# Row stores before the q and k loads, gate steps moved forward on VectorE, first weight loads on GpSimd's queue

## The chip, the cores and the metric

The program runs on one core of a Trainium2 chip. The metric is the device time of one execution in microseconds (us), as the median of several executions. A core has five engines that run their own instruction streams and meet only at semaphores: TensorE (PE in the profile: matmuls and transposes; PEld is its loading of weights), VectorE (DVE), ScalarE (ACT), GpSimd (POOL) and SyncE (SP, which does nothing here but read registers, branch and start DMAs). DMAs are started by SP and by POOL; SP's travel on one DMA queue, POOL's on another.

## The reference

Three layers follow each other. Sliding-window attention over 4 batches, 8 heads, 576 positions (heads 0 to 3 with a plain window of 32, heads 4 to 7 with a window of 128 dilated by 4); a mixture of 8 experts in which each of the 2304 tokens goes to the one expert with the highest logit; and a dense layer with a rational function between its two products.

```python
def _attn_ref(q, k, v):
    scores = scale * np.matmul(q, k.transpose(0, 1, 3, 2))
    scores = np.where(masks[None, :, :, :], scores, -1000000000.0)
    attn = np.exp(scores - np.max(scores, axis=-1, keepdims=True))
    attn = attn / (np.sum(attn, axis=-1, keepdims=True) + 1e-09)
    return np.matmul(attn, v)

def _moe_ref(x, modality_id, w_gate, modality_bias, w1, w2):
    logits = x @ w_gate + modality_bias[modality_id]
    e_idx = np.argmax(logits, axis=1)
    probs = softmax(logits)                      # gate_w = the chosen expert's share
    for e in range(8):
        mask = e_idx == e
        h = np.maximum(x[mask] @ w1[e], 0.0)
        out[mask] = gate_w[mask, None] * (h @ w2[e])
    return out

def _moe2_ref(x, w_in, w_out, a, b):
    h = x @ w_in
    P = a[0] + a[1] * h + a[2] * h**2 + a[3] * h**3
    Q = 1.0 + np.abs(b[0]) * np.abs(h) + np.abs(b[1]) * h**2
    return (P / (Q + 1e-06)) @ w_out
```

## The kernel before

**Order.** Instructions are written by hand in the order in which each engine runs them; the framework only adds the semaphores. What an engine finds blocked holds up everything behind it on that engine.

**Attention (`fused`).** Eight chunks of two heads by two batches (kinds dilated, dilated, plain, plain, twice) pass through 36 groups `g` of four tiles. For each group PE makes scores (`step_s`, tile `sc`), transposes the exponentials (`step_t`, `pt`) and multiplies them with v (`step_v`, `pv`, one PSUM buffer); VectorE divides and writes the rows into `xu` (L545). A tile `xu` holds two chunks, and there are two such tiles, so the first write of the third pair of chunks waits until every DMA that stores the first tile has read it. `load(c)` brings q and k of a chunk (`ldq`, `ldk`, two buffers each) by four DMAs on SP. `put_x` stores a finished `xu` to `x_rows` in DRAM: for a dilated pair of chunks by 20 small DMAs, which are put into the list `slow`; the loads of dilated v go into the list `first`. `issue(PACE)` at the end of each group starts up to four entries of the lists, those of `first` ahead. So the place of a store on SP, before or behind the four loads of the next chunk, is set by how many groups have passed.

**Experts (`moe`).** The tokens, sorted by expert, are run through slots of 128. A slot `s` gathers its rows on POOL (`gather`, L942, tiles `xg`), multiplies with w1 (`stage_1`, `p1t`), transposes (`stage_t`, `pht`) and multiplies with w2 (`stage_2`, `pot`); ScalarE's `put` scales `pot` by `gate` into `yo` and SP stores it to `ys_rows` (L1079). Matmuls are done in three products of high and low halves (`w1h`, `w1l` and so on). Where the expert changes between slots, `swap1` and `swap2` split new weights, the third quarter of each on POOL; where it doesn't, each engine walks past the branch. Three places of this part are in the change:

- Behind the fourth to eighth low half of w2 (`lo2`, list `lows`) VectorE writes the first two rows of the slot table `tab` (L974 to L1004). The generator `gates` (L951 to L969: 12 steps on VectorE and one on POOL, which make the three parts `ag` of the gate weights) is taken up step by step later, between the steps that write the rest of `tab` (L1251 to L1282). `followers` (L1285) comes behind these; then `gates_pe` (L1062) brings `ag` into slot order by 18 matmuls into `pyt` and VectorE combines them into `gate`. On PE these 18 stand behind 18 of the 24 matmuls of slot 2's first stage.
- Experts with few tokens left over are served at the side (`side`): their weights `sw` come by `side_fetch`, 8 DMAs of 256 KB for each matrix, and their rows go out by `side_put` (L1238), a scatter on POOL that waits for the latest store to `ys_rows`. Where `side_fetch` has nothing to fetch, SP, before it passes, waits until the eight semaphores over which its DMAs rotate have all been reached.
- The weights of the dense layer come as 64-bit numbers and are turned into 32-bit ones between slots (`narrow`, L1101: one ScalarE step and three VectorE steps for each of 32 pieces). `narrow_in` (L1094) loads a piece of 512 KB into `dr`, one of two buffers; the next piece is asked for as soon as VectorE has freed the buffer. All of these loads stand on SP.

**Dense layer (`second`).** 80 units of 512 columns; nothing in it is changed.

Of the kernel before, what the change touches and what calls it, by code (L numbers as in the profile page):

```python
# [2 lines left out]

# [9 lines left out]
I32 = mybir.dt.int32  # L13
# [152 lines left out]
def fused(ctx, tc, io):  # L166
# [214 lines left out]
    with ExitStack() as actx, tc.manual_schedule(), nc.allow_low_precision(reason="integers"):  # L381
# [24 lines left out]
        def load(c):  # L406
            bp, _, kind, h0 = CHUNKS[c]
            raw[c] = [ld.tile([72, 2, 2, 8 * D] if kind else [QT, 2 * NJ, 2, D], F32, tag="ld" + nm, name="ld" + nm) for nm in "qk"]
            bs = slice(2 * bp, 2 * bp + 2)
            if c == 0:  # L410
                for hh in range(2):
                    for t, src, eng in zip(raw[c], (q, k), (nc.sync, nc.scalar)):
                        eng.dma_start(out=t[:, hh], in_=src[bs, h0 + hh].rearrange("b (p j) d -> p b (j d)", j=8))
                    if hh == 0:
                        nc.sync.dma_start(out=ident, in_=io["cst"][:, 0:128])
                for lo, hi in ((0, 2), (2, NP0)):
                    nc.scalar.dma_start(out=mask[:, lo:hi], in_=io["mask"][:, lo:hi])
# [233 lines left out]
        for g in range(NG):  # L651
# [39 lines left out]
            if done_T == 4 * NU and not w1s:  # L691
# [7 lines left out]
                for n in range(2):  # L699
                    fetch2(n, e)  # L700
            if done_L < NC and done_T >= 8 * (done_L - 1):
                load(done_L)
                done_L += 1
            if done_V < done_L and TPG * (g - LAG2 + 1) >= 2 * NJ * (done_V // 2 * 2 - 2):
                load_values(done_V)
                first.append(lambda c=done_V: halo(c))
                done_V += 1
            issue(PACE)

        def split1(n, eng=nc.gpsimd):  # L710
            nonlocal nsp
# [35 lines left out]
def moe(ctx, tc, io, sh):  # L747
# [222 lines left out]

    gq = gates()
    lows = (lo2(c) for c in range(4, 8))
    cn = cd[0:1]
    nc.vector.tensor_tensor(out=cd[:, 0, :], in0=cnt, in1=nt[:, 0, :], op=ALU.min)  # L974
    next(lows, None)
    sd = st[0:1]
    S8 = [1, NS, 8]
    slot = C("slot")[0:1, 0:NS].rearrange("p (s o) -> p s o", o=1)
    wv = T([1, 1, 8], name="wv")
    nc.vector.scalar_tensor_tensor(out=wv, in0=cn, scalar=0.0, in1=nfe[0:1], op0=ALU.is_gt, op1=ALU.mult)  # L980
    next(lows, None)
    ge = T(S8, name="ge")
    es = T([1, NS, 1], name="es")
    nc.vector.memset(es[:, 0:1, :], 0.0)
    ge1 = ge[:, 1:]
    S7 = [1, NS - 1, 8]
    nc.vector.scalar_tensor_tensor(out=ge1, in0=slot[:, 0:NS - 1].to_broadcast(S7), scalar=128.0, in1=sd.to_broadcast(S7), op0=ALU.mult, op1=ALU.is_ge)
    next(lows, None)
    nc.vector.tensor_tensor(out=ge1, in0=ge1, in1=wv.to_broadcast(S7), op=ALU.mult)
    next(lows, None)  # L990
    nc.vector.tensor_reduce(out=es[:, 1:, 0], in_=ge1, op=ALU.max, axis=AX.X)
    next(lows, None)
    nc.vector.tensor_tensor(out=ge, in0=wv.to_broadcast(S8), in1=es.to_broadcast(S8), op=ALU.is_gt)
    next(lows, None)
    nc.vector.tensor_tensor(out=tab[:, 0, 0:NS - 1], in0=es[:, 1:, 0], in1=es[:, 0:NS - 1, 0], op=ALU.not_equal)
    next(lows, None)
    nc.vector.tensor_tensor(out=ge, in0=ge, in1=C("rev")[0:1, :].rearrange("p (o e) -> p o e", o=1).to_broadcast(S8), op=ALU.mult)
    next(lows, None)
    nx = T([1, NS], name="nx")
    nc.vector.tensor_reduce(out=nx, in_=ge, op=ALU.max, axis=AX.X)  # L1000
    next(lows, None)
    nc.vector.tensor_scalar(out=nx, in0=nx, scalar1=-1.0, scalar2=8.0, op0=ALU.mult, op1=ALU.add)
    next(lows, None)
    nc.vector.tensor_scalar(out=tab[:, 1, :], in0=nx, scalar1=7.0, scalar2=None, op0=ALU.min)  # L1004
    next(lows, None)
    run(lows)
    fill(slot1, 16 - FB)
    fill(second0, 8)
    run(slot1)
# [84 lines left out]
    def narrow_in(i):  # L1094
        qd, which, kk = i // 8, i // 4 % 2, i % 4
        w32[i] = pools["pa"].tile([128, 512], I32, tag="w" if i < 16 else "u", name=f"w32_{i}", bufs=17 if i < 16 else 16)
        r = pools["dp"].tile([128, 512, 2], I32, tag="dr", name="dr")
        nc.sync.dma_start(out=r, in_=srcs[which][qd, kk].bitcast(I32).rearrange("p (f w) -> p f w", w=2))
        nar[i] = r

    def narrow(chunks, ahead):  # L1101
# [147 lines left out]
    vs = T([1, NS], name="vs")  # L1249
    en = T([1, 1, 8], name="en")  # L1250
    nc.vector.tensor_tensor(out=en, in0=sd, in1=nt[0:1], op=ALU.add)  # L1251
    next(gq, None)
    nc.vector.tensor_reduce(out=tot, in_=en, op=ALU.max, axis=AX.XY)
    next(gq, None)
    nc.vector.tensor_scalar(out=vs, in0=slot[:, :, 0], scalar1=128.0, scalar2=tot, op0=ALU.mult, op1=ALU.is_lt)
    next(gq, None)
    nc.vector.tensor_copy(out=tab[:, 2, :], in_=vs)
    next(gq, None)
    nc.vector.scalar_tensor_tensor(out=ge, in0=slot.to_broadcast(S8), scalar=128.0, in1=sd.to_broadcast(S8), op0=ALU.mult, op1=ALU.subtract)
    next(gq, None)  # L1260
    nc.vector.scalar_tensor_tensor(out=ge, in0=ge, scalar=0.0, in1=cn.to_broadcast(S8), op0=ALU.max, op1=ALU.min)
    next(gq, None)
    cb = T([1, NS], name="cb")
    nc.vector.tensor_reduce(out=cb, in_=ge, op=ALU.add, axis=AX.X)
    next(gq, None)
    nc.vector.tensor_tensor(out=vs[:, 0:NS - 1], in0=cb[:, 0:NS - 1], in1=vs[:, 0:NS - 1], op=ALU.mult)
    next(gq, None)
    nc.vector.tensor_reduce(out=cb[:, NS - 1:], in_=vs[:, 0:NS - 1], op=ALU.max, axis=AX.X)
    next(gq, None)
    ct = T([128, 1, 8], name="ct")  # L1270
    nc.vector.tensor_tensor(out=ct[:, 0, :], in0=cnt, in1=cd[:, 0, :], op=ALU.subtract)
    next(gq, None)
    tt = T([1, 1], name="tt")
    nc.vector.tensor_reduce(out=tt, in_=ct[0:1, 0, :], op=ALU.add, axis=AX.X)
    next(gq, None)
    nc.vector.tensor_scalar(out=tab[:, 3, 0:2], in0=cb[:, 0:2], scalar1=tt, scalar2=None, op0=ALU.add)
    nc.vector.tensor_scalar(out=tab[:, 3, 2:], in0=cb[:, 2:], scalar1=tt, scalar2=hole[0:1], op0=ALU.add, op1=ALU.add)
    next(gq, None)
    nc.vector.memset(tab[:, 4, :], 0)
    nc.vector.tensor_scalar(out=tab[:, 4, 0:8], in0=ct[0:1, 0, :], scalar1=0.0, scalar2=None, op0=ALU.is_gt)  # L1280
    next(gq, None)
    nc.vector.tensor_reduce(out=tab[:, 4, 9:11], in_=tab[:, 4, 0:8].rearrange("p (c e) -> p c e", c=2), op=ALU.max, axis=AX.X)  # L1282
    next(gq, None)

    def followers():  # L1285
        tv, tq, tm = T([1, 1, 8], name="tv"), T([1, 8, 8], name="tq"), T([1, 8], name="tm")
# [389 lines left out]
```

## Time and profile before

| | |
|---|---|
| Executions timed | 823.46, 825.47, 827.88 us; median 825.47 us |
| Profiled execution | 818.36 us, of which the span from first to last instruction is 816.5 us |
| PE | 784.9 us busy, 96% of the span |
| DVE, ACT, POOL | 576.2 us (71%), 509.5 us (62%), 140.2 us (17%) |
| Mean granted TensorE clock | 0.984 of full speed |
| DMA | 91.60 MB; 69587 packets of SP's queue, 3360 of POOL's |

The rows below come from one profiled execution. In a timeline a row gives the start of an instruction, its duration, the engine, the line of the kernel, the operation and its tiles; the brackets give how long the engine had been idle before it and which event ended that. "SPq" and "POOLq" are the sequencers of these engines. The rows of windows give how long each engine was busy in a stretch, the granted clock of TensorE as a share of its full speed, the share of time in which the 16 DMA engines worked, and GB/s.

### The profile page before, as it was taken

The numbers are of one execution on the slowest core, as the hardware profiler recorded it, in microseconds if no ns is written. First come the engines' busy times: TensorE is split into PE (matmuls) and PEld (weight loads), VectorE is DVE, ScalarE is ACT, GpSimd is POOL, SyncE is SP. The second block draws the span as 40 slices with busy tenths as digits, with TensorE's granted clock in tenths as the row PEclk, the third lists the DMA queues.
The fourth block names the chain that finished last, engine by engine and source line by source line (L and its number), as shares of the span: only waits on it lengthen the run. The fifth ranks groups of instructions, "written<-read, shape, count | busy, mean of one in ns | idle before, by whom it ended". The sixth has DMA issues, their size and how long they took to land.

```text
span 816.5 us, 15443 instructions
## 1 busy us (share of the span) xinstructions
PE 784.9 (96%) x5297; PEld 636.8 (78%) x5299; DVE 576.2 (71%) x1389; ACT 509.5 (62%) x993; POOL 140.2 (17%) x181
## 2 busy tenths in 40 slices
PE   8998899989999999999899999999999999999995
PEld 4766666777776878888678888888888889999884
DVE  2776789742243235894599988888788788888894
ACT  3666567323343343664699877766777778778783
POOL 2030004131102002230366502000020002001001
PEclk7999899999999999999999999999999999999998
DMA  7988946479778947781011001100020001001001
GB/s 187 161 168 156 178 155 196 141 253 319 248 265 277 322 148 250 259 293 55 17 40 42 12 0 65 40 0 1 1 90 1 1 1 64 1 1 39 1 0 39
DMA packets 73654, 91.60 MB, mean 112 GB/s; under 512 B 33721, under 2 KB 43467, under 8 KB 73547
## 3 DMA queue, kind: packets, MB, share of 16 engines
q1 hardware_dynamic: 69587, 78.48, 33.5%
q0 software_dynamic: 3360, 11.03, 3.9%
q8 instruction: 49, 0.80, 0.4%
q10 hardware_dynamic: 600, 0.81, 0.4%
q14 instruction: 58, 0.48, 0.2%
HBM read 75.59 MB, written 14.71 MB: 111 GB/s over the span
## 4 chain that ended last, share of the span: by engine, by line
PE 66%; DVE 1%; ACT 1%; issue 1%; POOL 0%; POOLq 0%; ACTq 0%
PE p1t L1407 8%; PE p1t L1408 8%; PE p1t L1409 8%; PE pht L1578 4%; PE pht L1577 4%; PE pht L1579 4%; PE pot L797 3%; PE pot L799 2%; PE pot L795 2%; PE pot L1579 2%; PE p1t L149 2%; PE p1t L147 2%; PE p1t L145 2%; PE pxt L1577 2%; PE pxt L1578 2%; PE pxt L1579 2%
## 5 line engine op out<-in xcount | busy, mean ns | idle before, releaser
L1525 ACT ACTIVATE raw<-p1t 128x512 f32<-128x512 f32 (+1 forms) x78 | 43.2, 554 | 82.4 <-PE p1t L1409 82.4
L1532 DVE TENSOR_TENSOR raw<-raw,raw 128x512 f32<-128x512 f32 (+1 forms) x80 | 51.9, 648 | 58.4 <-ACT raw L1526 57.6
L1409 PE MATMUL p1t<-yh,wl 128*128 128x512 f32 (+1 forms) x240 | 88.9, 370 | 0.0
L788 DVE TENSOR_TENSOR hl<-pht,hh 128x512 fp32r<-128x512 f32 x34 | 21.9, 686 | 82.3 <-ACT hh L787 82.1
L1526 ACT ACTIVATE raw<-raw,bab 128x512 f32<-128x512 f32 (+1 forms) x80 | 61.9, 774 | 2.7
L1588 POOL DMA_INDIRECT out<-hs,row x10 | 10.8, 1084 | 302.1 <-ACT hs L1586 300.7
L1407 PE MATMUL p1t<-yh,wh 128*128 128x512 f32 (+1 forms) x160 | 59.6, 372 | 0.3 <-DVE m L1543 0.3
L1408 PE MATMUL p1t<-yl,wh 128*128 128x512 f32 (+1 forms) x160 | 59.2, 370 | 0.0
L1554 DVE SCALAR_TENSOR_TENSOR m<-m,nab,raw 128x512 f32<-128x512 f32 (+1 forms) x80 | 58.6, 733 | 0.1
L1552 DVE SCALAR_TENSOR_TENSOR raw<-raw,raw 128x512 f32<-128x512 f32 (+1 forms) x80 | 56.3, 704 | 0.0
L1527 ACT ACTIVATE raw<-p1t,nab 128x512 f32<-128x512 f32 (+1 forms) x78 | 56.1, 719 | 0.0
L145 PE MATMUL p1t<-w1h,xh 128*128 128x512 f32 x136 | 55.1, 405 | 0.0
L797 PE MATMUL pot<-w2l,hh 128*128 128x512 f32 x128 | 51.0, 399 | 3.2 <-POOLq L1037 3.2
L1534 ACT ACTIVATE raw<-raw,bab 128x512 f32<-128x512 f32 (+1 forms) x80 | 53.7, 671 | 0.4 <-DVE raw L1532 0.3
L147 PE MATMUL p1t<-w1l,xh 128*128 128x512 f32 x136 | 53.7, 395 | 0.3 <-DVEq L1029 0.3
L149 PE MATMUL p1t<-w1h,xl 128*128 128x512 f32 x136 | 53.8, 396 | 0.1
L1543 DVE SCALAR_TENSOR_TENSOR m<-m,nab,p1t 128x512 f32<-128x512 f32 (+1 forms) x78 | 53.4, 685 | 0.1
L1550 DVE SCALAR_TENSOR_TENSOR raw<-raw,raw 128x512 f32<-128x512 f32 (+1 forms) x80 | 52.7, 659 | 0.0
L1541 DVE TENSOR_TENSOR m<-raw,p1t 128x512 f32<-128x512 f32 (+1 forms) x78 | 49.3, 632 | 3.3 <-PE pdt L824 0.7
L795 PE MATMUL pot<-w2h,hh 128*128 128x512 f32 x128 | 51.5, 402 | 0.0
L799 PE MATMUL pot<-w2h,hl 128*128 128x512 f32 x128 | 50.2, 392 | 0.0
L1409 PEld LDWEIGHTS p1t<-yh,wl 128*128 128x128 f32 x240 | 45.0, 188 | 6.3
(391 smaller groups left out, 2083.7 us busy)
## 6 DMA issues: line engine op xcount, KB each, us to landing
sw<-in_w SPq DMA_DIRECT2D x80, 256.0 KB
raw<-in_w SPq DMA_DIRECT2D x12, 1024.0 KB
dr<-in_w_in SPq DMA_DIRECT2D x16, 512.0 KB
dr<-in_w_out SPq DMA_DIRECT2D x16, 512.0 KB
y<-ys_rows SPq DMA_DIRECT2D x18, 256.5 KB
ldq<-in_q SPq DMA_DIRECT2D x16, 288.0 KB
ys_rows<-yo SPq DMA_DIRECT2D x17, 256.5 KB
ldk<-in_k SPq DMA_DIRECT2D x14, 288.0 KB
```

The costliest lines, as they stand in the source:

```text
L145: nc.tensor.matmul(out=p, lhsT=xh[:, kk], rhs=wh[n][:, kk], start=(kk == 0), stop=False)
L147: nc.tensor.matmul(out=p, lhsT=xh[:, kk], rhs=wl[n][:, kk], start=False, stop=False)
L149: nc.tensor.matmul(out=p, lhsT=xl[:, kk], rhs=wh[n][:, kk], start=False, stop=(kk == 3))
L795: nc.tensor.matmul(out=p, lhsT=a[:, c], rhs=w2h[n][:, kk], start=(c == 0), stop=False)
L797: nc.tensor.matmul(out=p, lhsT=a[:, c], rhs=w2l[n][:, kk], start=False, stop=False)
L799: nc.tensor.matmul(out=p, lhsT=b[:, c], rhs=w2h[n][:, kk], start=False, stop=(c == 7))
L1407: nc.tensor.matmul(out=p[:, 0:n], lhsT=wh(kk)[:, cs], rhs=ab[0][:, kk, 0:n], start=(kk == 0), stop=False)
L1408: nc.tensor.matmul(out=p[:, 0:n], lhsT=wh(kk)[:, cs], rhs=ab[1][:, kk, 0:n], start=False, stop=False)
L1409: nc.tensor.matmul(out=p[:, 0:n], lhsT=wl(kk)[:, cs], rhs=ab[0][:, kk, 0:n], start=False, stop=(kk == 3))
L1526: nc.scalar.activation(out=v, in_=ah, func=AF.Identity, scale=bab[:, 1:2], bias=bab[:, 0:1])
L1554: nc.vector.scalar_tensor_tensor(out=m, in0=m, scalar=nab[:, 0:1], in1=v, op0=ALU.add, op1=ALU.mult)
L1579: nc.tensor.matmul(out=o, lhsT=gl[:, cs], rhs=wa, start=False, stop=(f == 15))
```

## The change

Four edits, in three places.

- In attention, when the next chunk's q and k are about to be loaded and at most `FLUSH` = 5 entries are left in `slow`, all entries of both lists are started first. And a group in which both lists have entries starts six of them and not four.
- The generator `gates` is chained behind the last low halves of w2, so its steps stand between the steps that write the first two rows of `tab`; the rest of it follows right behind them. The later steps of `tab` are left alone among themselves. `ct` is computed at the start.
- `narrow_in` starts the loads of pieces 0 to 15 on POOL's queue; pieces 16 to 31 stay on SP.

```diff
+FLUSH = 5
...
             if done_L < NC and done_T >= 8 * (done_L - 1):
+                if len(slow) <= FLUSH:
+                    issue(len(first) + len(slow))
                 load(done_L)
...
-            issue(PACE)
+            issue(PACE + 2 if first and slow else PACE)
...
     gq = gates()
     lows = (lo2(c) for c in range(4, 8))
+    both = iter(chain(lows, gq))
+
+    def more():
+        next(both, None)
+
     cn = cd[0:1]
     nc.vector.tensor_tensor(out=cd[:, 0, :], in0=cnt, in1=nt[:, 0, :], op=ALU.min)
-    next(lows, None)
+    ct = T([128, 1, 8], name="ct")
+    nc.vector.tensor_tensor(out=ct[:, 0, :], in0=cnt, in1=cd[:, 0, :], op=ALU.subtract)
+    more()
...
-    next(lows, None)
-    run(lows)
+    more()
+    run(both)
...
-        nc.sync.dma_start(out=r, in_=srcs[which][qd, kk].bitcast(I32).rearrange("p (f w) -> p f w", w=2))
+        (nc.gpsimd if i < 16 else nc.sync).dma_start(out=r, in_=srcs[which][qd, kk].bitcast(I32).rearrange("p (f w) -> p f w", w=2))
...
     nc.vector.tensor_tensor(out=en, in0=sd, in1=nt[0:1], op=ALU.add)
-    next(gq, None)
     nc.vector.tensor_reduce(out=tot, in_=en, op=ALU.max, axis=AX.XY)
-    next(gq, None)
...
-    run(gq)
     followers()
     gates_pe()
```

On SP, in attention, the 20 stores of the first `xu` stand with the loads of the sixth and seventh chunk. Near the end of these stores the order was, before:

```order
L437 DMA x_rows<-xu 64x256
L437 DMA x_rows<-xu 48x256
L425 DMA ldq<-in_q 64x18x64 x2
L425 DMA ldk<-in_k 64x18x64 x2
L437 DMA x_rows<-xu 16x256
L437 DMA x_rows<-xu 64x2x256
L609 DMA x_rows<-xu 64x9x256 x2
```

and is now:

```order
L439 DMA x_rows<-xu 64x256
L439 DMA x_rows<-xu 48x256
L439 DMA x_rows<-xu 16x256
L439 DMA x_rows<-xu 64x2x256
L427 DMA ldq<-in_q 64x18x64 x2
L427 DMA ldk<-in_k 64x18x64 x2
L611 DMA x_rows<-xu 64x9x256 x2
```

The last two stores of the tile have moved in front of the four loads. In the same way the loads of the chunk before, which stood behind the third of the 20 stores, now stand behind the ninth.

On VectorE, where the later rows of `tab` are written (`g`, `pc` and `ag` belong to the gates, the others to the table), the order was, before:

```order
L955 TENSOR_SCALAR g<-g 128x18
L1255 TENSOR_SCALAR vs<-cst,tot 1x26
L957 RECIPROCAL g<-g 128x18
L1257 CAST tab<-vs 1x26
L961 CAST pc_2905<-g 128x18
L1259 SCALAR_TENSOR_TENSOR ge<-cst,st 1x208
L964 TENSOR_TENSOR g<-g,pc_2905 128x18
```

and the same steps of the gates now stand earlier, among the steps of the table's first rows, ahead of `xl` of slot 2:

```order
L959 TENSOR_SCALAR g<-g 128x18
L1006 TENSOR_TENSOR tab<-es 1x25
L961 RECIPROCAL g<-g 128x18
L1008 TENSOR_TENSOR ge<-ge,cst 1x208
L965 CAST pc_2751<-g 128x18
L1011 TENSOR_REDUCE nx<-ge 1x26
L968 TENSOR_TENSOR g<-g,pc_2751 128x18
```

All 12 steps of the gates on VectorE have moved so. The one on POOL moves with them: it stood behind the branch of `swap1(2)`, and now stands between the gathers of slots 2 and 3.

On POOL, at the end of slot 3, the order was, before:

```order
L1037 COMPARE_AND_BRANCH
L130 TENSOR_TENSOR w2l_2526<-raw_2304,w2h_2524 128x512
L130 TENSOR_TENSOR w2l_2527<-raw_2305,w2h_2525 128x512
L1037 UNCONDITIONAL_BRANCH x2
L1015 TENSOR_LOAD tab
L942 DMA xg_70<-x_rows,idx 128x512
```

and is now:

```order
L1048 COMPARE_AND_BRANCH
L132 TENSOR_TENSOR w2l_2526<-raw_2304,w2h_2524 128x512
L132 TENSOR_TENSOR w2l_2527<-raw_2305,w2h_2525 128x512
L1048 UNCONDITIONAL_BRANCH x2
L1109 DMA dr<-in_w_in 128x1024 x2
L1026 TENSOR_LOAD tab
L946 DMA xg_70<-x_rows,idx 128x512
```

Two loads of `dr` now stand on POOL between the branch of `swap2` and the next slot's gather; they are gone from the same place on SP. This is so in seven slots.

## Rows read from the trace of the kernel before

**Rows 1.** Waits of PE: for whom, us in total, times, longest
```profile
PE p1t L1408 <- issue: 3.1, 1, 3.1
```

**Rows 2.** Timeline of DVE in attention, the first write of the third `xu`
```profile
83.41 0.42 DVE L545 TENSOR_TENSOR xu<-pv,rs 128x256 f32<-128x256 f32 x1 [6.76 <-DMA x_rows<-xu]
```

**Rows 3.** Timeline of PE in attention: products with v, a later use of q
```profile
72.72 0.69 PE L531 MATMUL pv<-vw,pts 96*64 96x65 f32 x16
...
75.38 0.69 PE L531 MATMUL pv<-vw,pts 96*64 96x65 f32 x16
...
83.94 1.13 PE L531 MATMUL pv<-vw,pts 96*64 96x65 f32 x16 [5.30 <-issue]
...
88.38 0.69 PE L531 MATMUL pv<-vw,pts 96*64 96x65 f32 x16
...
93.22 0.52 PE L479 MATMUL pq<-ident,ldq 64*128 64x64 f32 x5
```

**Rows 4.** Windows: engines' busy us, then PEclk, DMA share and GB/s
```profile
84.00:88.00 4.00, 4.00 (x43) 3.48 (x44) 2.62 (x20) 1.94 (x6) 0.00 (x0) 0.50 0.98 240
```

**Rows 5.** Timeline of SP's DMA starts in attention
```profile
56.97 2.03 SPq L437 DMA_DIRECT2D x_rows<-xu  x3
59.11 0.78 SPq L423 DMA_DIRECT2D ldq<-in_q  x2
...
61.96 10.60 SPq L437 DMA_DIRECT2D x_rows<-xu  x15
...
77.86 2.43 SPq L437 DMA_DIRECT2D x_rows<-xu  x2
```

**Rows 6.** Timeline of PE around the gate matmuls
```profile
163.36 0.39 PE L149 MATMUL p1t<-w1h,xl 128*128 128x512 f32 x1
166.65 1.71 PE L1065 MATMUL pyt<-ag,bm 128*128 128x99 f16 x18 [2.90 <-DVE ag L968]
168.14 0.78 PE L145 MATMUL p1t<-w1h,xh 128*128 128x512 f32 x1
...
170.80 0.48 PE L795 MATMUL pot<-w2h,hh 128*128 128x512 f32 x1
```

**Rows 7.** Timeline of DVE in the same place
```profile
158.61 0.69 DVE L139 TENSOR_TENSOR xl<-pxt,xh 128x512 fp32r<-128x512 f32 x1 [4.03 <-ACT xh L137]
...
160.80 0.15 DVE L1251 TENSOR_TENSOR en<-st,nt 1x8 f32<-1x8 f32 x1
...
166.59 0.14 DVE L1287 SCALAR_TENSOR_TENSOR tv<-ct,cst 1x8 f32<-1x8 f32 x1
...
168.92 0.20 DVE L1070 SCALAR_TENSOR_TENSOR gate<-gs 128x33 f32<-128x33 f32 x1
```

**Rows 8.** Timeline of ACT (first `put`)
```profile
169.15 0.69 ACT L1076 ACTIVATE yo<-pot,gate 128x512 f32<-128x512 f32 x1 [6.06 <-DVE gate L1070]
```

**Rows 9.** Tile `xg`, stretch 145 to 170: time from a gather's start to its landing
```profile
DMA to landing us min/median/max: 3.3/4.8/5.2
```

**Rows 10.** Timeline of all engines around the stall at 243.6
```profile
234.18 0.39 PE L797 MATMUL pot<-w2l,hh 128*128 128x512 f32 x1
234.41 0.39 PE L799 MATMUL pot<-w2h,hl 128*128 128x512 f32 x1
...
234.84 0.69 ACT L1076 ACTIVATE yo<-pot,gate 128x512 f32<-128x512 f32 x1 [4.79 <-PE pot L799]
...
236.29 1.30 SPq L1098 DMA_DIRECT2D dr<-in_w_out  x2
...
243.68 0.36 SPq L1079 DMA_DIRECT2D ys_rows<-yo  x1
...
246.69 1.00 POOL L1238 DMA_INDIRECT ys_rows<-sdy,goal  x1 [27.89 <-DVEq L1029]
246.85 0.50 PE L797 MATMUL pot<-w2l,hh 128*128 128x512 f32 x1 [3.22 <-POOLq L1037]
```

**Rows 11.** List of waits, SP
```profile
SPq L1098 <- DVE w L1113: 16.5, 12, 3.9
```

More of the change, by code (lines that the diff above doesn't have):

```diff
@@ L1 @@
+from itertools import chain
 import numpy as np
@@ L987, in moe @@
     nc.vector.scalar_tensor_tensor(out=ge1, in0=slot[:, 0:NS - 1].to_broadcast(S7), scalar=128.0, in1=sd.to_broadcast(S7), op0=ALU.mult, op1=ALU.is_ge)
-    next(lows, None)
+    more()
     nc.vector.tensor_tensor(out=ge1, in0=ge1, in1=wv.to_broadcast(S7), op=ALU.mult)
-    next(lows, None)
+    more()
     nc.vector.tensor_reduce(out=es[:, 1:, 0], in_=ge1, op=ALU.max, axis=AX.X)
-    next(lows, None)
+    more()
     nc.vector.tensor_tensor(out=ge, in0=wv.to_broadcast(S8), in1=es.to_broadcast(S8), op=ALU.is_gt)
-    next(lows, None)
+    more()
     nc.vector.tensor_tensor(out=tab[:, 0, 0:NS - 1], in0=es[:, 1:, 0], in1=es[:, 0:NS - 1, 0], op=ALU.not_equal)
-    next(lows, None)
+    more()
     nc.vector.tensor_tensor(out=ge, in0=ge, in1=C("rev")[0:1, :].rearrange("p (o e) -> p o e", o=1).to_broadcast(S8), op=ALU.mult)
-    next(lows, None)
+    more()
     nx = T([1, NS], name="nx")
     nc.vector.tensor_reduce(out=nx, in_=ge, op=ALU.max, axis=AX.X)
-    next(lows, None)
+    more()
     nc.vector.tensor_scalar(out=nx, in0=nx, scalar1=-1.0, scalar2=8.0, op0=ALU.mult, op1=ALU.add)
-    next(lows, None)
+    more()
     nc.vector.tensor_scalar(out=tab[:, 1, :], in0=nx, scalar1=7.0, scalar2=None, op0=ALU.min)
-    next(lows, None)
-    run(lows)
+    more()
+    run(both)
     fill(slot1, 16 - FB)
@@ L1251, in moe @@
     nc.vector.tensor_tensor(out=en, in0=sd, in1=nt[0:1], op=ALU.add)
-    next(gq, None)
     nc.vector.tensor_reduce(out=tot, in_=en, op=ALU.max, axis=AX.XY)
-    next(gq, None)
     nc.vector.tensor_scalar(out=vs, in0=slot[:, :, 0], scalar1=128.0, scalar2=tot, op0=ALU.mult, op1=ALU.is_lt)
-    next(gq, None)
     nc.vector.tensor_copy(out=tab[:, 2, :], in_=vs)
-    next(gq, None)
     nc.vector.scalar_tensor_tensor(out=ge, in0=slot.to_broadcast(S8), scalar=128.0, in1=sd.to_broadcast(S8), op0=ALU.mult, op1=ALU.subtract)
-    next(gq, None)
     nc.vector.scalar_tensor_tensor(out=ge, in0=ge, scalar=0.0, in1=cn.to_broadcast(S8), op0=ALU.max, op1=ALU.min)
-    next(gq, None)
     cb = T([1, NS], name="cb")
     nc.vector.tensor_reduce(out=cb, in_=ge, op=ALU.add, axis=AX.X)
-    next(gq, None)
     nc.vector.tensor_tensor(out=vs[:, 0:NS - 1], in0=cb[:, 0:NS - 1], in1=vs[:, 0:NS - 1], op=ALU.mult)
-    next(gq, None)
     nc.vector.tensor_reduce(out=cb[:, NS - 1:], in_=vs[:, 0:NS - 1], op=ALU.max, axis=AX.X)
[L1269 to L1272, printed above, removed]
     tt = T([1, 1], name="tt")
     nc.vector.tensor_reduce(out=tt, in_=ct[0:1, 0, :], op=ALU.add, axis=AX.X)
-    next(gq, None)
     nc.vector.tensor_scalar(out=tab[:, 3, 0:2], in0=cb[:, 0:2], scalar1=tt, scalar2=None, op0=ALU.add)
     nc.vector.tensor_scalar(out=tab[:, 3, 2:], in0=cb[:, 2:], scalar1=tt, scalar2=hole[0:1], op0=ALU.add, op1=ALU.add)
-    next(gq, None)
     nc.vector.memset(tab[:, 4, :], 0)
     nc.vector.tensor_scalar(out=tab[:, 4, 0:8], in0=ct[0:1, 0, :], scalar1=0.0, scalar2=None, op0=ALU.is_gt)
-    next(gq, None)
     nc.vector.tensor_reduce(out=tab[:, 4, 9:11], in_=tab[:, 4, 0:8].rearrange("p (c e) -> p c e", c=2), op=ALU.max, axis=AX.X)
-    next(gq, None)
     def followers():
```

## The prediction

> **What bounds the kernel now.** The page's first part, the share of each engine, comes first: PE is busy for 784.9 of 816.5 us. So a change can gain only what PE stands still, some 30 us, or what it does at a lowered clock. The chain of waits is mostly PE too, so the next view is the list of PE's own waits, and then the timelines around each. The list has four waits over 2 us. One, 3.1 us at the start of the dense layer, is put down to "issue" [rows 1]; no edit touches it. The other three are where the edits are.
>
> First, 5.30 us in attention: a product with v waits [rows 3] because VectorE stood for 6.76 us before the first write of the third `xu` [rows 2], and what ended that was a DMA that stores the first `xu`. Second, 2.90 us ahead of the gate matmuls, ended by VectorE's last `ag` [rows 6]. Third, 3.22 us inside an expert slot, before a product with `w2l`, put down to POOL's branch [rows 10].
>
> **Edit 1, the stores.** Nothing is added or removed; SP's order is changed. Before, the 20 stores of the tile were started as 3, then four loads, then 15, then four loads, then 2, and these last two started between 77.86 and 80.29 [rows 5]. Behind 256-byte loads they had to wait for the DMA engines, too, and the write went on at 83.41, at most 3.1 us after the last start.
>
> Now nine stores go first. A store costs SP 0.71 us (15 in 10.60), so they end at 56.97 + 9 x 0.71 = 63.4. The four loads of the sixth chunk took 59.11 to 61.96, that is 2.85: 66.2. Eleven stores: 74.0. With the same 3.1 us to landing the tile is free at 77.1. VectorE is ready to write at 83.41 - 6.76 = 76.65; PE is ready for its next product at 83.94 - 5.30 = 78.64 and needs the write, 0.42 long, ended. So VectorE waits some 0.5 us and PE not at all, with a margin of 1 us. The 5.30 us go in full.
>
> After the stall the granted clock was 0.50 from 84 to 88, the lower level, 1.2 GHz [rows 4]. From one product with v to the next it took 88.38 - 83.94 = 4.44 us there, against 75.38 - 72.72 = 2.66 for the same work before the stall [rows 3]. Without the stall nothing lowers the clock: another 1.78 us. **Edit 1 takes 7.1 us.** Its bounds are 0 (the stores land as late as before) and some 7.5 (a part of the next group was slow as well).
>
> What is late next: the seventh chunk's q and k. Their loads start at 74.0 in place of 72.6. The stores that stood behind them landed by 83.4, so I take the loads to be there by about the same time, now 84.8. Their first use, at 93.22, comes forward to 86.1. That is close but covered; if the cover fails, each us of lateness costs one.
>
> **Edit 2, the gates.** Between the first table step at 160.80 and the first step of `followers` at 166.59 [rows 7] VectorE did 28 instructions in 5.79 us; 13 of these are gone from there (12 of the gates and `ct`). The 15 that stay are 0.08 to 0.36 us long and follow each other closely; their durations add up to 3.05 us, which I take. So `followers` begins 2.74 us earlier, at 163.85, and ends as much earlier; and since `ag` is ready before, VectorE no longer waits 0.23 us for PE behind it. `gate`, which ended at 169.12, ends at 166.15.
>
> On PE the 18 gate matmuls follow directly on the eighteenth of the stage, at 163.6 and not at 166.65. They took 1.49 us to the next instruction, 168.14 - 166.65 [rows 6], at a lowered clock; at full clock it is between half of that and all of it, and I take the middle, 1.1. Six matmuls at 0.23 (the distance of two in [rows 10]) and four transposes of some 0.1 follow: PE is at `pot` at 166.5. But `pot` must first be read by ScalarE's `put`, which waits for `gate` [rows 8]: 166.2 + 0.69 = 166.9. So PE begins `pot` at 166.9 in place of 170.80: **3.9 us**, the clock's part in it included. The stall isn't wholly gone; some 0.4 us of it turns into a wait for `put`, and VectorE's table steps are what is late next. Bounds: 0 and 4.4.
>
> Where the moved steps go: VectorE stood idle for 4.03 us ahead of slot 2's `xl` at 158.61 [rows 7]. Six of the twelve steps slip between dependent table steps, and some 2.5 to 3.5 us of the rest lie in that gap, so `xl` is hardly moved. The first rows of `tab` come some 0.5 us later and with them SP's loads of the next expert, which nobody needs for 100 us. On POOL the gate product goes ahead of slot 3's gather; it waits for VectorE until about 156, and the gather, which had followed that of slot 2 at once, starts at about 157.5. With a landing of 5.2 us at most [rows 9] it is there at 163, and PE wants it at 166. Cost 0.
>
> **Edit 3, the weight loads.** The stall at 243.6 is a chain. PE wants the part of `w2l` that is POOL's, so POOL must have passed the branch of `swap2`; POOL stood at the scatter of `side_put` until 246.69; the scatter must follow the store to `ys_rows`, started on SP at 243.68 only [rows 10]. Its data had been in `yo` since 235.5. SP had been waiting at a `side_fetch` with nothing to fetch, where it passes only after all its eight semaphores have been reached; among these were the two `dr` loads of 236.29. With them on POOL's queue SP waits only for side weights that were started earlier. I put the store at 237 to 241; 3.0 us later (246.69 - 243.68) the scatter starts and 0.2 later PE goes on: 240 to 244, PE asking at 243.6. **3.2 us**, between 2.8 and 3.2; 0 if SP waits for the side weights just as long.
>
> What is added on POOL: 16 loads, 2 in each of seven slots and two at the start. A start of a DMA takes POOL 1.0 us [rows 10], so 2 us for each slot of 11 us and more (48 matmuls at 0.23). They wait for VectorE to free `dr`: on SP 16.5 us over 12 waits, 3.9 at most [rows 11]. Behind them on POOL stand the next gather, needed one slot later, and the branches of `swap1` and `swap2`, which PE asks for a slot later. Cost 0. The Trainium skill, DMA: Bandwidth & Descriptors, section Issuing engine by pattern, puts plain loads on SyncE as the generally faster issuer. The trace agrees for the starts: 0.65 us each for SP's two at 236.29, 1.0 for POOL's. By the rule the sum loses 16 x 0.35 = 5.6 us of POOL's time, and none of PE's, since POOL is idle for four fifths of the span.
>
> **The sum.** 7.1 + 3.9 + 3.2 = 14.2 us. The profiled execution took 818.36, so 804.2 for that one. The median of the timed ones, 825.47, is 0.9% above it; I take the same 14.2 off: **811.3 us**.
>
> **Rivals.**
> - *The attention stall stays, or comes back as a late load.* For it: the DMA engines work for 0.98 of the time there [rows 4] and 7 us less are left for the same bytes. Against: the 1 us of margin above. Edits 2 and 3 alone give 7.1: 818.4.
> - *The gates gain nothing*, because slot 3's gather lands late among the loads of 4 MB, or because VectorE's table steps take as long alone. Edits 1 and 3: 815.2.
> - *SP's wait stays with the side weights.* The `dr` loads now share the DMA engines with them and don't queue behind them. Then edit 3 gives 0: 814.5. Two loads of 0.5 MB at the 240 GB/s of [rows 4] would put off the side weights by up to 4.4 us; if PE has to wait that long for them once, on top of the stall that stays, it is 818.9. The Trainium skill, the same page, section Queues, rings and completion order, says that each DMA engine takes turns between queues, which is this rival; no row here shows turns.
> - *Slower: POOL is late at each slot.* If its waits for `dr` make it pass `swap2` later than PE asks, each of seven slots pays what the stall of [rows 10] shows, 3.2 us: 22.4, less 7.1 + 3.9 makes +11.4: 836.9. It decides when POOL is held for more than the 11 us or so between a slot's narrowing and PE's asking; the longest wait was 3.9.
> - *The change doesn't do what it says.* The order of the stores and steps shows that it does; what could remain is nothing gained at all, 825.5.
>
> **How the numbers follow.** Forecast with all three 0.62; attention rival 0.12; gates rival 0.08; side weights 0.09; slower 0.04; nothing 0.05. All but the last two are faster than 821.3, which is 0.5% (what measurements of this kernel can tell from no change): faster 0.90 by these, and I move 0.02 to within 0.5% for two partial failures at once: faster 0.88, within 0.07, slower 0.05. The range runs from 806.5 (the upper bounds, and a base at the lowest timed run) to 818.9, the far end of the rivals that are faster: they and the forecast make 0.88 or so of the chance, and single runs differ by 2 us.
>
> **What would show it.** Edit 1: no DMA wait over 1 us before VectorE's `xu`, the clock at 1.00 where it was 0.50, and the last store of the tile started near 74. Wrong if PE waits for `ldq` of the seventh chunk at 86. Edit 2: the 18 gate matmuls directly behind the stage's eighteenth; ScalarE's `put` 3 us earlier; a wait of about 0.4 us before `pot`. Wrong if PE waits for `xg`. Edit 3: no wait for POOL's branch in the middle of a slot, and the store to `ys_rows` within 2 to 5 us of `yo`. Wrong if PE waits for `sw`, or for POOL in several slots.

## The result and the profile after

| | kernel before | with the change |
|---|---|---|
| median of 4 runs | 824.64 us | 814.47 us (813.01 to 826.55) |
| ratio, with its 95% interval | 1 | 0.9865 (0.9822 to 0.9908) |
| profiled execution, its span | 818.36, 816.5 us | 813.22, 811.4 us |

Executions at a lowered clock, as the highest of the four (826.55), are left out of every ratio. The kernel is faster by some 11 us (7.6 to 14.7 by the interval). The forecast was 811.3 us, or a ratio of 0.9828; the time lies in its range, and the sign and most of the size are right. But the parts don't add up as they were meant to, and one part did not happen.

The waits of PE in the changed kernel (for whom, us in total, times, longest) show it at once:

```profile
PE pot L801 <- POOLq L1048: 4.4, 1, 4.4
PE pot L1571 <- ACT gh L1553: 2.0, 1, 2.0
PE pdt L1238 <- DMA sw<-in_w: 1.7, 1, 1.7
...
PE px L137 <- DMA xg<-x_rows,idx: 1.7, 1, 1.7
```

The waits at the product with v and ahead of the gate matmuls are gone. The 3.2 us inside a slot, which edit 3 was to remove, are there and are 4.4 us long. The wait at the start of the dense layer [rows 1], which no edit was to touch, is gone too.

**Attention.** Three groups of rows answer [rows 2 to 5]: PE's products with v, VectorE's write of the third `xu`, and SP's starts.

```profile
73.22 0.69 PE L533 MATMUL pv<-vw,pts 96*64 96x65 f32 x16
...
76.43 0.69 PE L533 MATMUL pv<-vw,pts 96*64 96x65 f32 x16
...
79.09 0.69 PE L533 MATMUL pv<-vw,pts 96*64 96x65 f32 x16
```

```profile
75.86 0.42 DVE L547 TENSOR_TENSOR xu<-pv,rs 128x256 f32<-128x256 f32 x1 [1.36 <-DMA x_rows<-xu]
```

```profile
65.54 6.50 SPq L439 DMA_DIRECT2D x_rows<-xu  x6
71.57 2.31 SPq L439 DMA_DIRECT2D x_rows<-xu  x4
73.98 1.43 SPq L427 DMA_DIRECT2D ldq<-in_q  x2
```

The last store now starts before 73.9, VectorE waits 1.36 us and no longer 6.76, and PE goes from one product with v to the next without a stall. The wait of 1.36 us is over the 1 us that the prediction had named as its limit. The granted clock of PE, 0.50 from 84 to 88 us before [rows 4], is 1.00 (columns: busy us of the engines, then PEclk, DMA share, GB/s):

```profile
76.00:80.00 4.00, 4.00 (x73) 3.38 (x73) 3.89 (x25) 2.81 (x9) 0.00 (x0) 1.00 1.34 181
84.00:88.00 4.00, 4.00 (x71) 3.14 (x71) 3.75 (x21) 2.80 (x9) 0.00 (x0) 1.00 1.05 279
```

**The gates.** PE's timeline around the gate matmuls, against [rows 6], and ScalarE's first `put`, against [rows 8]:

```profile
155.82 0.39 PE L151 MATMUL p1t<-w1h,xl 128*128 128x512 f32 x1
156.05 1.27 PE L1076 MATMUL pyt<-ag,bm 128*128 128x99 f16 x18
157.14 0.48 PE L147 MATMUL p1t<-w1h,xh 128*128 128x512 f32 x1
...
159.70 0.49 PE L799 MATMUL pot<-w2h,hh 128*128 128x512 f32 x1 [0.51 <-ACT yo L1087]
```

```profile
158.63 0.69 ACT L1087 ACTIVATE yo<-pot,gate 128x512 f32<-128x512 f32 x1 [3.09 <-DVE gate L1081]
```

The gate matmuls follow the eighteenth matmul directly, take 1.09 us (1.1 was the forecast), and the wait before `pot` is 0.51 us (0.4 was).

**The slot.** The chain of [rows 10] again, in the changed kernel, from ScalarE's `yo` over SP's store and POOL's scatter to PE:

```profile
222.38 2.73 SPq L1201 DMA_DIRECT2D sw<-in_w  x5
...
223.79 0.69 ACT L1087 ACTIVATE yo<-pot,gate 128x512 f32<-128x512 f32 x1 [4.78 <-PE pot L803]
...
233.91 0.36 SPq L1090 DMA_DIRECT2D ys_rows<-yo  x1
...
236.84 1.01 POOL L1249 DMA_INDIRECT ys_rows<-sdy,goal  x1 [12.92 <-SPq L1198]
...
237.00 0.80 PE L801 MATMUL pot<-w2l,hh 128*128 128x512 f32 x1 [4.40 <-POOLq L1048]
```

`yo` is complete at 224.48, and its store starts 9.4 us later (8.2 before: 235.5 to 243.68). No `dr` load stands on SP here any more, and SP is as late as it was. Its waits between 224 and 234.5 all stand at branches whose body it skips, L1048 (`swap2`), L1040 (`swap1`) and L1198 (`side_fetch`):

```profile
SPq L1048 <- SPq L1048: 2.3, 2, 2.1
SPq L1198 <- SPq L1198: 1.8, 3, 0.7
SPq L1040 <- SPq L1040: 1.4, 2, 1.1
```

The updates of the DMAs' semaphores in the trace tell what it waits for: the side weights, of which the eighth, started at 224.71, has landed at 232.62. Before, the eighth was started at 234.94 and had landed at 239.96, and SP waited last for the two `dr` loads behind it, which landed at 241.27 and 242.51. From 225 to 231 the DMA engines work at a share of 1.00 and 352 GB/s. Besides the side weights they move 0.52 MB of POOL's queue, two gathers; the `dr` loads that POOL had started had landed by 225.44.

```profile
225.00:231.00 6.00, 6.00 (x32) 5.06 (x31) 4.64 (x8) 3.07 (x6) 0.00 (x0) 1.00 1.00 352
```

### The profile page after: what moved, and what is told of

It is laid out like the page before. It is cut to its first block, busy times and chain, and to the rows that moved or that the text cites. A ratio compares the mean times of both kernels' runs of the same rounds, so it can differ in the third digit from the quotient of the medians.

```text
span 811.4 us, 15423 instructions
## 1 busy us (share of the span) xinstructions
PE 785.2 (97%) x5297; PEld 636.1 (78%) x5299; DVE 574.8 (71%) x1389; ACT 508.8 (63%) x993; POOL 145.0 (18%) x197
## 4 chain that ended last, share of the span: by engine, by line
PE 48%; ACT 2%; DVE 1%; POOL 0%; issue 0%; POOLq 0%; ACTq 0%
PE p1t L1401 8%; PE p1t L1402 8%; PE p1t L1403 8%; PE pht L1571 4%; PE pht L1572 4%; PE pht L1573 4%; PE pot L1573 2%; PE pot L1571 2%; PE pxt L1571 2%; PE pot L1572 2%; PE pxt L1572 2%; PE pxt L1573 2%; ACT raw L1520 0%; PE pdt L1386 0%; PE pyt L1386 0%; DVE raw L1526 0%
## 5 line engine op out<-in xcount | busy, mean ns | idle before, releaser
L1402 PE MATMUL p1t<-yl,wh 128*128 128x512 f32 (+1 forms) x160 | 59.3, 371 | 0.0
```

The source lines that it names most:

```text
L1402: nc.tensor.matmul(out=p[:, 0:n], lhsT=wh(kk)[:, cs], rhs=ab[1][:, kk, 0:n], start=False, stop=False)
```

## Where the time went, stretch by stretch

One trace of each kernel is not enough, since the kernel before varies. Its second profile (among the runs below) has the same stalls, longer. So the table measures, on PE's timeline of each run, the distance between six points: the start of the third `lgp` product (69 to 71 us, in the ninth line 85), of the first `pr`, of the first `pyt<-oh,upper`, of the first `pyt<-ident,sdy`, of the twelfth `pxt<-ident,xg`, of the third group of `pht<-wl,gh`, and the end of the span. Stretch A holds the attention stall, B the first gather, C the gates, D the slots with side work, E the way into the dense layer, F the rest. In the labels, "late" is a move of POOL's scatter that the experiments bring in.

| run | A | B | C | D | E | F |
|---|---|---|---|---|---|---|
| before, first profile | 27.9 | 42.7 | 41.7 | 124.1 | 123.5 | 385.8 |
| before, second profile | 31.3 | 43.0 | 41.6 | 127.0 | 125.8 | 385.8 |
| edit 3 alone | 33.4 | 42.7 | 41.7 | 129.3 | 121.5 | 387.1 |
| edit 1 alone | 21.1 | 44.7 | 41.9 | 127.5 | 123.9 | 385.8 |
| edits 1 and 2 | 21.1 | 44.6 | 38.1 | 128.7 | 124.8 | 385.8 |
| all three, first profile | 20.7 | 44.5 | 38.1 | 129.7 | 122.5 | 387.1 |
| all three, second profile | 21.2 | 43.9 | 38.2 | 129.4 | 122.5 | 387.1 |
| all three, late | 20.9 | 45.9 | 38.1 | 126.3 | 122.8 | 387.1 |
| edits 1 and 2, late | 21.1 | 42.8 | 38.1 | 125.2 | 126.4 | 385.8 |
| edits 1 and 2 and two loads of edit 3, late | 21.5 | 43.6 | 38.2 | 125.7 | 126.1 | 386.0 |

For the two second profiles, which ran on one chip: 10.1 - 0.9 + 3.4 - 2.4 + 3.3 - 1.3 = 12.2, against 823.7 - 811.7 = 12.0 us of span. Edit 1 brings 6.4 to 12.7 us in A by which profiles are set side by side, and up to 3.2 of it go back in B. Edit 2 brings 3.4 to 3.8 in C, in every pair. Wherever all of edit 3 is in, D is longer than in the kernel that differs by it alone, and E is shorter.

## The experiments

**Each edit alone, and edits 1 and 2.** The edits of the change are put into the kernel before one at a time; the last kernel is the changed one with this line put back:

```
-        (nc.gpsimd if i < 16 else nc.sync).dma_start(out=r, in_=srcs[which][qd, kk]...
+        nc.sync.dma_start(out=r, in_=srcs[which][qd, kk]...
```

Edit 1 (`FLUSH`, `PACE + 2`) alone:

> The kernel before with edit 1 alone (the order of the row stores). Forecast: 7.1 us off, so a ratio of 0.9914 against the kernel before, the last store of the tile started near 74 us, no stall of PE at the product with v, the granted clock at 1.00 from 76 to 88 us. Rival (late loads of the seventh chunk): PE waits for ldq near 86 us and the ratio is above 0.996. The side weights' theory (below) says nothing else here than the forecast.

Measured: 816.98 us, ratio 0.9898 (0.9865 to 0.9931), that is 8.4 us of 825. PE waits 0.27 us at the product with v; in A 21.1 us against 27.9 and 31.3. PE waited for q and k only in the first 18 us, so the rival of late loads falls. It is more than the 7.1 us of the forecast, whose ratio, 0.9914, lies within the interval.

Edit 2 (`both = chain(lows, gq)`, `ct` early) alone:

> The kernel before with edit 2 alone (gate steps ahead of slot 2's low half). Forecast: 3.9 us off, ratio 0.9953, the gate matmuls directly behind the eighteenth matmul of the stage and a wait of about 0.4 us before pot. Rival (slot 3's gather late): PE waits for xg one slot later and the ratio is 0.998 or more.

Measured: 823.29 us, ratio 0.9958 (0.9926 to 0.9989), 3.5 us. It is the size of the forecast and of stretch C in the other runs, though the interval reaches from 0.9 to 6.1 us and does not rule out the rival's 0.998 by itself. Its profiled execution took 1925.67 us, so no row of its trace is used; in the traces with edits 1 and 2 PE does not wait for slot 3's gather.

Edit 3 (16 loads of `dr` on POOL's queue) alone:

> The kernel before with edit 3 alone (16 weight loads from SP to POOL). Forecast: the stall of 3.2 us inside the slot goes, ratio 0.9961. Side weights' theory: SP still passes its empty side fetch only when the side weights in flight have landed, now slower because the dr loads of the other queue share the DMA engines; the stall stays at 3 us or more, PE may wait for sw as well, and the kernel is between 0 and 6 us slower: ratio 1.000 to 1.007.

Measured: 826.98 us, ratio 1.0037 (0.9998 to 1.0076): no gain, and more likely some 3 us lost. The waits of PE in that kernel:

```profile
PE pv L531 <- issue: 8.8, 1, 8.8
PE pot L797 <- POOLq L1037: 4.4, 1, 4.4
...
PE pdt L1227 <- DMA sw<-in_w: 1.4, 2, 0.7
```

The stall behind POOL's branch stays, at 4.4 us, and waits for the side weights come on top. That is the rival of the side weights, which had been given a chance of 0.09.

Edits 1 and 2 without edit 3:

> Edits 1 and 2 without edit 3. Forecast: 7.1 + 3.9 = 11.0 us off, ratio 0.9867, which is 3.2 us slower than all three edits together. Side weights' theory: edit 3 gives nothing or costs up to 6 us, so this kernel is as fast as all three edits or up to 6 us faster (ratio 0.980 to 0.987 where all three had 0.9865).

Measured: 815.43 us, ratio 0.9897 (0.9854 to 0.9941). The ratio lies 0.003 above that of all three edits in the first measurement and 0.0065 above that in the second (below), 2.6 and 5.4 us, with intervals that overlap, so no gain of edit 3 is shown here. By the table it comes to nearly nothing: the slots are no shorter by it (the stall is 5.4 us here and 4.4 with edit 3, but the whole of D is 128.7 against 129.4 and 129.7), E is 2.3 us shorter, and F 1.3 us longer.

**Both kernels again.**

> The kernel before again, one look, to see how its stalls vary from one execution to another: the one in attention was 5.3 us in the first profile, and 8.8 us in that of the kernel with edit 3 alone, whose code is the same up to there. If it is 7 to 9 us here, edit 1 is worth more than the 7.1 us of the forecast in most executions; the 3.1 us at the start of the dense layer shall show whether that one comes and goes by itself.

Measured: one execution of 825.54 us. Its waits of PE:

```profile
PE pv L531 <- issue: 6.6, 1, 6.6
PE pot L797 <- POOLq L1037: 4.7, 1, 4.7
...
PE p1t L1408 <- issue: 2.8, 1, 2.8
```

All three are the stalls of the first profile, and the first two are 1.3 and 1.5 us longer. More than that comes behind the first: the clock stays at 0.50, the lower level of 1.2 GHz, until 92 us and not until 88.

```profile
80.00:92.00 12.00, 8.30 (x83) 6.16 (x85) 5.09 (x28) 2.65 (x8) 1.28 (x2) 0.50 1.01 212
```

> The kernel with all three edits again, on the chip on which the two kernels with the moved store run. Forecast of the record: ratio 0.9828; the first measurement had 0.9865. By its profile the three edits gave 7.1, 3.5 and nothing, so 10.6 us of 825, less what the later waits for a gather, the side weights and POOL took back: ratio 0.985 to 0.990.

Measured: 819.84 us as the median of all 12 executions, ratio 0.9832 (0.9785 to 0.9879), and 813.58 us for the profiled execution. Its profile has the 4.2 us stall at `pot` and 1.9 us of waits for `sw`, as the first had 4.4 and 1.7.

**The store ahead of the side fetch.** SP meets the empty side fetch ahead of the store; here the two change places:

```
         else:
             side(e)
-            side_fetch(e + 1, 0)
         put(pot, gate[:, s:s + 1], idx[:, s:s + 1], s)
+        if e is not None:
+            side_fetch(e + 1, 0)
```

> All three edits, and on SP the store to ys_rows now stands ahead of the side fetch instead of behind it. SP theory (the stall at pot is POOL's scatter behind a store that SP held back at an empty side fetch, until the side weights in flight had landed): the store follows yo by 2 us, no wait of PE for POOL's branch inside a slot, and the 4.4 us of that stall with some 1.2 us of lowered clock behind it go: 5.6 us less than the three edits alone, some 807.6 where they had 813.2. If the scatter waits for something else (the DMA engines, the side weights themselves), the stall stays and the time is that of the three edits within 1 us.

Measured: 839.31 us, ratio 1.0153 (1.0093 to 1.0213).

> Edits 1 and 2 without edit 3, with the store to ys_rows ahead of the side fetch on SP. SP theory: the 5.4 us stall of edits 1 and 2 goes, about 6 us less than those two alone (ratio 0.982 against the kernel before, where those two had 0.990). It also prices edit 3 without the stall: if the dr loads on POOL's queue only slow the side weights, this kernel is faster than the one of all three edits with the same move by 0 to 2 us; if POOL's queue is the better place, slower by 1 to 3 us.

Measured: 828.58 us, ratio 0.9982 (0.9944 to 1.002). Both expectations failed: by the ratios 26 and 7 us slower than without the move (1.0153 against 0.9832, 0.9982 against 0.9897). The waits of PE, with all three edits:

```profile
PE pdt L1226 <- SPq L1199: 9.5, 2, 4.9
PE pdt L1226 <- DMA sw<-in_w: 5.0, 3, 2.9
PE pot L801 <- POOLq L1048: 4.4, 1, 4.4
```

A fetch that is not empty now has to wait for `yo`, which is complete only at the end of the slot, and the side weights come too late. In the kernel of edits 1 and 2 the second fetch starts at 182.70 on SP; with the move, in an execution that is 3.8 us later at this place, it starts behind the store of 190.42:

```profile
190.42 0.35 SPq L1090 DMA_DIRECT2D ys_rows<-yo  x1
192.50 4.97 SPq L1202 DMA_DIRECT2D sw<-in_w  x8
```

PE then waits 4.21 us for them at 214.38. I had taken the first half of a fetch to be released only with the slot's end; it is released earlier. As the 4.4 us stall came back behind loads that were themselves late, the kernel says nothing on what holds the store. Even with the loads in time the move could not have won all of it: in the changed kernel SP comes to that fetch at 230.7 only, behind its waits at `swap2` and `swap1`, so by an estimate the store would have started there, some 3 us earlier. The kernel shows that the side fetch, not the store, is the more urgent of the two on SP.

**The scatter behind the branch.** Here SP is left alone, and only POOL's order is changed: the scatter of `side_put` goes behind the branch of `swap2`, for which PE waits.

```
-        if e in (3, 7):
-            side_put(e // 4)
...
         swap2(s)
         if s < P0:
             narrow(STEPS[s - 3][0:2], len(STEPS[s - 3]))
+        if e in (3, 7):
+            side_put(e // 4)
```

> All three edits, and side_put (POOL's scatter to ys_rows) moved behind the branch of swap2 and the slot's dr loads; SP is left as it is. Theory: PE waits for POOL's branch only because POOL stands at the scatter, which waits for a store that SP starts late. Then the stall of 4.2 to 4.4 us at pot goes, with the lowered clock behind it (some 1.2 us): 5.5 us off the three edits, 807.7 where those had 813.2, ratio 0.977. What may be late next: the side weights (PE waited 1.7 to 1.9 us for them before; up to 4 us more if they set the pace), which would leave 1 to 2 us of gain. Rival (POOL is held by something else, or PE is held by ScalarE's or VectorE's part of the weights): stall and time stay.

Measured: 811.62 us, ratio 0.9881 (0.9833 to 0.9928). No wait for POOL's branch is left, though the scatter is started as late as ever, at 239.65:

```profile
239.65 1.03 POOL L1249 DMA_INDIRECT ys_rows<-sdy,goal  x1 [6.06 <-SPq L1198]
```

So the end of the chain is as read: PE waited for POOL's branch, and POOL stood at the scatter. D is 3.1 to 3.4 us shorter than with all three edits. The gain was larger on the way: the fourth side product starts 78.7 us after the first `pyt<-ident,sdy`, against 85.0 and 85.6, so 6.3 to 6.9 us were won up to there. Behind it PE waits for side weights, as the expectation feared (the wait put down to SP ends with one too, started at 251.69 and landed at 260.25), while the DMA engines have a share of 1.03 and move 388 GB/s (waits of PE, its timeline, a window):

```profile
PE pdt L1238 <- SPq L1048: 2.0, 1, 2.0
...
PE pdt L1238 <- DMA sw<-in_w: 0.9, 3, 0.5
```

```profile
260.29 0.43 PE L1238 MATMUL pdt<-sw,sdt 128*32 128x128 f32 x8 [1.97 <-SPq L1048]
```

```profile
255.00:260.00 5.00, 3.31 (x21) 2.24 (x21) 0.00 (x0) 0.77 (x2) 0.00 (x0) 1.00 1.03 388
```

> Edits 1 and 2 without edit 3, with side_put behind the branch of swap2. Theory as for the kernel with all three: the 5.4 us stall goes, some 6.6 us with the clock, ratio 0.982 where edits 1 and 2 alone had 0.990. Against the kernel of all three edits with the same move it prices edit 3 where no scatter holds POOL: by the record's theory of edit 3 (a shorter way for SP) both are alike; by the side weights' theory this one loses less to waits for sw, by some 1 to 2 us, and keeps the 3 us at the start of the dense layer that no kernel with edit 3 has shown so far: 1 to 2 us slower in all.

Measured: 810.83 us, ratio 0.9847 (0.9818 to 0.9876). The stall behind POOL is gone here too, D is 3.5 us shorter than without the move, and PE's wait for the DMA of `sw` is 0.2 us in all. In place of the stall PE waits 1.9 us for ScalarE's `sdx`, and once 1.4 us for SP. The 3.1 us at the start of the dense layer are there, as the expectation had them.

**Two loads of the sixteen.** The kernel of all three edits with the late scatter, and of edit 3 only the last two loads:

```
-        (nc.gpsimd if i < 16 else nc.sync).dma_start(...
+        (nc.gpsimd if 14 <= i < 16 else nc.sync).dma_start(...
```

> Edits 1 and 2, side_put behind the branch of swap2, and of edit 3 only the last two of the 16 loads (14 and 15, started in the last of the seven slots) on POOL's queue, the other 14 on SP. Two things are told apart. First, the side weights: with 14 of the loads on SP, PE should wait for sw no more than without edit 3 (under 2 us in all, against 2.9 us and a lowered clock with all 16 on POOL). Second, the 3 us of PE at the start of the dense layer, which stood in all six kernels without edit 3 (0.8 to 3.4) and in none of the five with it: if it hangs on those loads of the early slots, it is back here; if any load on POOL's queue is enough, or the place of the code in PE's program, it may stay away. With both good, some 808 us where all three edits had 813; with the stall back, some 810.

Measured: 812.36 us, ratio 0.9848 (0.9798 to 0.9898). The waits of PE:

```profile
PE p1t L1402 <- issue: 3.1, 1, 3.1
PE pdt L1225 <- DMA ys_rows<-yo: 2.8, 1, 2.8
...
PE pdt L1238 <- DMA sw<-in_w: 0.2, 1, 0.2
```

The wait for the side weights' DMA falls from 0.9 (and 2.0 more behind SP) to 0.2: with the early `dr` loads on POOL's queue, beside the side weights and not behind them, the side weights are slower. But 2.8 us of another wait have come. It is put down to the last of several semaphores, a store's; PE goes on at 237.84, 0.05 us after ScalarE has ended `sdx`, and ScalarE had stood 6.95 us for a `dr` load that SP had queued behind the side weights:

```profile
233.53 0.69 ACT L1117 ACTIVATE w<-dr 128x512 f32<-128x512 f32 x1 [6.95 <-SPq L1198]
...
237.19 0.60 ACT L1211 ACTIVATE sdx<-pyt 128x512 f32<-128x512 f32 x1 [0.19 <-ACTq L1040]
```

The 1.9 us of the kernel without edit 3 come the same way (ScalarE stands 5.93 us for `dr`). So with the scatter out of the way some 3 us of waits are left on either queue: for the side weights with all the `dr` loads on POOL's, behind ScalarE's `dr` with these loads on SP's. And the dense layer's stall is back.

The three kernels with the late scatter have ratios of 0.9847 to 0.9881, and the changed kernel 0.9832 and 0.9865. These are not told apart by their intervals; none is shown to beat the change.

## Why the prediction came out as it did

- **The bound** was read rightly: PE's own stalls are what there is to gain.
- **Edit 1, forecast 7.1.** Its steps hold, with less to spare than it said. Between the two first profiles the stretch is shorter by 7.1 us (27.86 to 20.74). Stores were to end near 74.0 (73.88), VectorE to wait 0.5 us (1.36), PE not at all. But in this execution VectorE is ready 2.15 us earlier than before (74.50 against 76.65), and SP's stores are not; of the margin of 1 us, 0.15 is left between the end of the write (76.28) and PE's product (76.43). In other traces with the edit VectorE waits up to 2.1 us and PE up to 0.7. The seventh chunk's q is first used at 83.94, without a wait. Mis-sized is the base: the first profile held a short stall. In the two later traces with the old order it is 6.6 and 8.8 us, the clock is low for longer, and the stretch is 10 to 13 us longer than after. What was not foreseen is B: PE waits 1.7 us for a gather in the profile of the change (0.4 before), 1.8 in those of edit 1 and of edits 1 and 2. In the second profile of the change it waits 0.4 there, and 1.5 for an `xu`.
- **Edit 2, forecast 3.9**, measured 3.4 to 3.8 by the table and 3.5 by the times. The half microsecond is the step from `put` to `pot`: PE starts 0.38 us after the end of ScalarE's `put` (158.63 + 0.69 = 159.32, `pot` at 159.70), which the working had set to nothing. The `xl` of slot 2 did not move, as forecast: 151.09 against 158.61, and the stage before it is as much earlier. Slot 3's gather starts at 151.07, and PE doesn't wait for it at 158.60.
- **Edit 3, forecast 3.2: wrong.** The step that failed is "With them on POOL's queue SP waits only for side weights that were started earlier. I put the store at 237 to 241". The chain behind the store was right (the late scatter shows it), and so was the load that SP waited for last. Without the two kernels with the moved store there are six traces with these `dr` loads on SP, and in each they land 2.5 to 3.8 us after the last side weight. What failed is that the side weights would land as early without them. From the start of the eighth side weight ahead of that store to its landing it is 4.4 to 5.0 us in these six traces, and 7.9 to 8.2 in the four with all of edit 3; to the landing of the last load of either kind it is 7.6 to 8.8 us in the six, against the same 7.9 to 8.2. The edit changed which load lands last, and hardly when. That is the rival of the side weights. With edit 3 alone D is 2.3 us longer than in the longer, 5.2 than in the shorter profile of before; with edits 1 and 2 in, 0.7 to 1.0. The Trainium skill, DMA: Bandwidth & Descriptors, section Queues, rings and completion order, has each DMA engine take turns between queues; by that rule the loads of two queues slow each other, and the traces agree as far as these landings go. That the rule is the reason was not measured apart.
- **POOL's price for the loads** was too high: 1.0 us for each was taken from an indirect DMA, the scatter of [rows 10]. A start of `dr` takes 0.53 to 0.59 on POOL. SP's 0.65 was read too high as well: the 1.30 us of that pair hold a wait of 0.5 for a semaphore, and a pair that need not wait takes 0.84 (the start at 218.78). PE did not wait for POOL on their account. But POOL stands at them for VectorE much longer than the 3.9 us that were taken from SP's list (its sequencer 12.3 us before the load of 218.25), and two gathers behind them fall onto the side weights (with edits 1 and 2 alone they start at 196.76 and 203.68). Whether the `dr` loads or these gathers slow the side weights more was not parted.

```profile
218.25 0.54 POOL L1109 DMA_DIRECT2D dr<-in_w_out  x1 [13.29 <-DVE w L1124]
219.57 0.53 POOL L1109 DMA_DIRECT2D dr<-in_w_out  x1 [0.78 <-ACTq L1220]
221.29 1.02 POOL L1205 DMA_INDIRECT sdy<-x_rows,sidx  x1 [1.19 <-issue]
222.61 0.98 POOL L946 DMA_INDIRECT xg<-x_rows,idx  x1 [0.31 <-PE pot L803]
```

- **The sum** of 14.2 is thus 11 to 12 by compensation, and that the time lies so near the forecast is luck in part: more from edit 1 in two of the three traces with the old order, 0.5 less from edit 2, nothing in the slots where 3.2 were forecast and 2.4 lost there, and 3.3 less 1.3 in the dense layer that nobody forecast (2.3 of the 3.3, and the 1.3, go with edit 3). D grows with edits 1 and 2 as well (127.5 and 128.7): PE comes to the slots some 10 us earlier (first `pyt<-ident,sdy` at 172 to 174 us, against 183 and 185), and presumably the transfers of the slots can't be as much faster. Among the chances, the four cases called faster add up to 0.91, not 0.90.

## What to carry to other kernels

A stall behind a queue of DMA starts ends with whichever load in the queue comes last. Taking that kind of load off it helps only if the others then still land as early; here they landed some 3 us later beside the moved loads, with the DMA engines at a share of 1.00, and the last landing stayed where it was. And a wait that one engine has for another's branch was cut here at the link next to the waiting engine (the scatter moved behind the branch) and not three links back; even then only 3.1 to 3.4 of the 6.3 to 6.9 us won on the way were kept, as the next transfer in line was late. Before a stall is priced from one trace, see how long it is in a second one: here the same stall was 5.3, 6.6 and 8.8 us.

## What the runs showed that was not expected

**The start of the dense layer.** PE's wait put down to "issue" is 3.1 and 2.8 us in the two profiles of before, 2.3 with edit 1, 3.4 with edits 1 and 2, 3.1 with the late scatter without edit 3 and with two loads of it, and 0.8 with the store moved and edit 3 left out. In all five traces (of four kernels) with the whole of edit 3 it is 0.3 or less. The place with edits 1 and 2, and with all three:

```profile
385.33 0.47 PE L1401 MATMUL p1t<-yh,w1h 128*128 128x512 f32 x1 [0.30 <-issue]
389.25 0.59 PE L1402 MATMUL p1t<-yl,w1h 128*128 128x512 f32 x1 [3.45 <-issue]
```

```profile
384.71 0.47 PE L1401 MATMUL p1t<-yh,w1h 128*128 128x512 f32 x1 [0.47 <-ACT hh L791]
385.02 0.40 PE L1402 MATMUL p1t<-yl,w1h 128*128 128x512 f32 x1
```

PE waits there for nothing that the profile shows and does nothing. It comes to this place over a branch (the end of the slots, which depends on the data). The Trainium skill, Runtime: NRT & Kernel Launch, section Instruction fetch mechanics, says that a taken branch to code that isn't at hand makes the engine wait for that code's load; that would look like this. The trace agrees in part: in the stall of edits 1 and 2, from 385.80 to 389.25, the DMA queues that carry instructions move one block of 16 KB and three of 8 KB, the first from 385.89, the last until 388.38; with all three edits the like starts at 385.27 only, behind L1402, and PE doesn't wait. Whose code these blocks hold the trace doesn't tell. Why 14 loads on another queue 150 us earlier change it no run here tells: whether by the place of the code or by what else is under way then stays open. Part of it goes back at once, as PE then waits 2.0 us for `gh` in place of 0.8 to 1.3.

**The end.** With all of edit 3 the span ends 1.3 us later behind the same last work (F: 387.1 against 385.8). The last wait on SP, which is put down to PE's sequencer, is 1.3 us longer in the second profile of the change than in that of before:

```profile
SPq L1672 <- PEq L1672: 1.9, 2, 1.3
```

```profile
SPq L1666 <- PEq L1666: 3.1, 2, 2.6
```

Its cause was not looked for.
